# Folding batch 4's columns one step later: a limit table at the meeting of the transform stage and the expert slots

## Chip, cores and metric

One core of a Trainium2 chip runs the whole program. The metric is device time in microseconds (us), the median of several executions of the same kernel on the same inputs. An engine's queue is the list of its instructions in the order in which it takes them: PE (TensorE), DVE (VectorE), ACT (ScalarE), POOL (GpSimd) and SP (SyncE, which here only issues DMAs).

## What is computed

```python
def _attn_ref(x):                       # x: 8 batches of 2496 x 256
    X = np.fft.fft(x, axis=1)
    X = np.fft.fft(X, axis=2)
    return X.real.astype(np.float32)

def _moe_ref(x, w_gate, w_output_gate, w1, w2):   # x: the 19968 rows of the transform
    logits = x @ w_gate
    e_idx = np.argmax(logits, axis=1)             # one of 8 experts for each row
    ...
    for e in range(E):
        h = np.maximum(x[mask] @ w1[e], 0.0)
        ye = h @ w2[e]
        out[mask] = gate_w[mask, None] * eom[mask, e, None] * ye
```

The real part of a two-dimensional Fourier transform of each batch gives 2496 rows of 256. A gate picks one expert of eight for every row, and the expert is a two-layer network (256 to 1024 to 256).

## The kernel before

**The transform stage.** A batch's input comes as five column chunks, numbered m = 5 * batch + chunk (the code's `divmod(m, KC)`, KC = 5). Each chunk is a tile `xt` of 512 KB, loaded by SP (L310). `fold1` (L419) adds the two halves of a chunk in place. It runs on DVE for batches 0 to 3 and on POOL from batch 4 on; from batch 5 on it has two more POOL instructions (L424, L425). `fold2` then makes sums and differences on DVE: a difference `ft<-xt` (L437), a sum in place `xt<-xt` (L441), and for chunks 1, 3 and 4 two more (L450, L452). After L452 the tiles are free again and `load_x` puts the load of a later chunk into SP's queue. For batches from 4 on, `fold2` follows `fold1` two chunks later (FLAG = 2).

The steps of the transform are numbered n = 5 * batch + i. A step has `sstage` (L556 on PE, into PSUM tiles `psb_t`), then the call of `folds` that the change touches, then `sevac`, which reads the step's PSUM tile out: ACT writes `qb` (L580), DVE writes `eo` (L582) and `rt` (L587). Within some steps `dstage`/`devac` (L492, L504, L505) prepare the next batch. Rows of the finished transform go to a scratch array in HBM by scatters of POOL (L705).

**The slots.** The experts run in slots of up to 256 rows. A slot has four rounds: `mm1` (12 matmuls L1282 into a PSUM tile `hp`, then ACT `hh` L1286 and DVE `hl` L1287, the slot's subtraction) and, three rounds later, `mm2` (L1304 into `yp`). `hp` has two buffers, so the matmuls of a round wait for the `hl` of two rounds before. A slot's rows come by SP: a transposing load `xr` (L1214) and a small one `xf` (L1215). Its weights come as `raw0b`, `raw1b` (L1224) and are converted by ACT and DVE (L1258, L1259).

**How the two meet.** Steps n = 0 to 14 are written out ahead of the first slot (FSTART = 14). From step 15 on the steps are a background, cut into pieces that are drawn between the pieces of slots. In the background `fold2` is told to come behind the newest slot's subtraction (`behind("DVE")`), and it is interleaved with the gating of the previous batch. When step 14 is written the PSUM pools of the transform are closed, and the pools of the slots (`hp`, `yp`) take over the same PSUM. So the first `mm1` waits until step 14's `sevac` has read its PSUM tile.

SP and POOL take their instructions in the order in which the program writes them. The order on PE, DVE and ACT is set by the framework's scheduler, within what dependencies and a few pins allow; the folds ahead of the first slot are pinned in the program's order.

**The line that changes** is the call of `folds` at L1115. Its second argument is the last chunk to be folded in step n, the smallest of three limits. The third is a table, read by n - 10:

```python
min(KC * (b + 1) + AHEAD[i], KC + 3 * n + 2,
    KC * (BA + 1) + (1, 4, 5, 6, 9, 99)[min(n - 5 * BA, 5)])
```

With BA = 2 the table's base is 15, the first chunk of batch 3. Ahead of the first slot, a limit of 20 in step 12, 21 in step 13 and 24 in step 14 lets all five `fold1` of batch 4 (chunks 20 to 24) and the `fold2` of its first three chunks be issued there.

Of the kernel before, what the change touches and what calls it, by code (L numbers as in the profile page):

```python
# [19 lines left out]
KC = 5  # L20
# [21 lines left out]
BA = BAS[0]  # L42
# [26 lines left out]
AHEAD = (5, 6, 7, 8, 9)  # L69
# [164 lines left out]
def fft_moe_kernel(ctx: ExitStack, tc: tile.TileContext, xl, wg, w1, w2, tde, tdo, gt, ts0, tsm, tsr, tsq, cst, tid, out):  # L234
# [47 lines left out]
    if True:  # L282
# [18 lines left out]
        def load_x(n=NB * KC):  # L301

            while n and len(xq) < xcap[0]:
                q = pw if held[pw] < NX2 and len(xq) < 2 * KC else px
                if held[q] == (NX2 if q is pw else NX):
                    break
                held[q] += 1
                b, c = divmod(len(xq), KC)
                t = q.tile([128, 8, HN], F32, name="xt", tag="xt", bufs=NX2 if q is pw else NX)
                nc.sync.dma_start(t, xl[b, c])  # L310
                xts[b, c] = t
                xq.append(q)
                n -= 1
# [85 lines left out]
        def weave(*gs):  # L399
            gs = list(gs)  # L400
            while gs:
                for g in list(gs):
                    try:
                        next(g)
                    except StopIteration:
                        gs.remove(g)
# [4 lines left out]
        def fold1(b, c, eng):  # L411
            x = xts[b, c][:, :, 0:KW[c]]
            if b == 0:

                sq = pw.tile([128, 8, 128], mybir.dt.bfloat16, name="sq0", tag="sq0", bufs=1)
                nc.scalar.activation(sq[:, :, 0:KW[c]], x, AF.Square, scale=4.0, accum_out=en0[:, c:c + 1])
            v = x.rearrange("p (h a b) n -> p h a b n", h=2, a=2)
            x0, x1 = x[:, 0:4], x[:, 4:8]
            i = eng.tensor_tensor(x0, x0, x1, op=ALU.add)  # L419
            if b < LB:  # L420
                if eng is nc.vector:
                    pin(i)
                return
            eng.tensor_tensor(v[:, 1, 0], v[:, 0, 0], v[:, 0, 1], op=ALU.add)  # L424
            eng.tensor_tensor(v[:, 1, 1], v[:, 0, 0], v[:, 0, 1], op=ALU.subtract)  # L425
# [520 lines left out]
        def add_gen(g):  # L946
            gens.append([g, next(g)])
# [54 lines left out]
        def folds(n, last, fillers=None):  # L1002
            while fq[0] <= last:
                m = fq[0]
                fq[0] += 1
                dve = m // KC <= BA + 1
                if m < NB * KC:
                    fold1(*divmod(m, KC), nc.vector if dve else nc.gpsimd)
                while fq[1] < NB * KC and fq[1] <= m - (0 if fq[1] // KC <= BA + 1 else FLAG):
                    f = fold2(*divmod(fq[1], KC))  # L1010
                    fq[1] += 1
                    if n < 5 * BA or fillers is None:
                        weave(f)
                    else:
                        fillers.append(f)
# [31 lines left out]
        def scales(b):  # L1047
            smalls.clear()
            for fn in (energy, energy_sum, scale):
                fn(b)  # L1050

        def steps():
            pinned.append(1)
            folds(0, 2 * KC - 1)
            xcap[0] = NB * KC
            load_x()
            gatepass(0)
            add_gen(gating(0))
            for _ in sstage(0, 0):
                pass  # L1060
            weave(piece("C"), sevac(0, 0))
            scales(1)
            for m in range(2):
                for h in range(2):
                    load_w(0, m, h)
            weave(piece("A"))
            fa = foldall(BA)
            weave(piece("C"), dparts(1))
            weave(piece("C"))
            some(fa, 12)  # L1070
            for n in range(5 * BA):
                b, i = divmod(n, 5)
                if n:
                    for _ in sstage(b, i):
                        pass
                    for _ in sevac(b, i):
                        pass
                send(b, i)
                some(fa, 3 if n < 2 else 99)
                if n == 2:  # L1080
                    fq[:] = 2 * [KC * (BA + 1)]
                    gatepass(1)
                    add_gen(gating(1))
                ahead((0, 0, 8, 12, 99)[min(n, 4)])
                if n == 4:
                    for _ in table_a(0):
                        pass
                if n in (1, 2):
                    for h in range(2):
                        wenergy(0, n - 1, h)  # L1090
                if n == 4:
                    for m in range(2):
                        wscale(sched[0][1], m)
                if n > 7:
                    conv(0, 0, n - 8)
                yield ("step", n)
            for n in range(5 * BA, 5 * NB):
                b, i = divmod(n, 5)
                if i == 0 and b > BA:
                    add_gen(gating(b - 1))  # L1100
                smalls.clear()
                if n == 5 * BA:
                    hold.append(1)
                    scales(BA)
                    for c in range(KC):
                        dstage(BA, c)
                        devac(BA, c)
                ds_ = ((), (), (0, 1), (2, 3), (4,))[i] if b > BA else ((), (), (), (0, 1, 2), (3, 4))[i]
                for c in ds_ if b + 1 < NB else ():
                    dstage(b + 1, c)  # L1110
                    devac(b + 1, c)
                    yield "d"
                yield from sstage(b, i)
                fillers = [piece("C")] if i or b > BA else []
                folds(n, min(KC * (b + 1) + AHEAD[i], KC + 3 * n + 2, KC * (BA + 1) + (1, 4, 5, 6, 9, 99)[min(n - 5 * BA, 5)]), fillers)  # L1115
                weave(*fillers)
                yield "s"
                sv = sevac(b, i)
                next(sv)
                for _ in sv:  # L1120
                    pass
                if n == 5 * BA:
                    for h in range(2):
                        conv(0, 1, h)
                if i == 1 + (b == BA) and b + 1 < NB:
                    energy(b + 1)
                    energy_sum(b + 1)
                    scale(b + 1)
                weave(piece("A"))
                yield ("step", n)  # L1130
            add_gen(gating(NB - 1))
            while gens:
                for _ in piece("C"):
                    yield "g"
                yield "g"
                weave(piece("A"))
                yield "g"
# [400 lines left out]
```

## Time and profile before

| what | value |
|---|---|
| median of 3 runs | 1090.22 us (1090.05 to 1091.33) |
| the profiled execution | 1091.5 us |
| its span, first to last instruction | 1089.6 us |
| PE busy | 1035.8 us, 95% |
| DVE busy | 662.7 us, 61% |
| POOL busy | 419.8 us, 39% |
| mean granted TensorE clock | 0.983 |

Busy time is the time in which an engine works on an instruction. A row of a timeline has the start in us, the duration in us, the engine, the line and operation, the tiles written and read, the shapes, how many instructions it joins, and in brackets the idle time of the engine just before it with what ended that. Timelines join neighbours, so that a joined row's duration reaches from its first start to its last end. The granted clock is 1.00 at 2.4 GHz and 0.50 at 1.2 GHz.

### The profile page before, as it was taken

Reading aid. Unit: us, or ns where it says so; the run is one execution under the profiler, and the core shown is the slowest. Engines: PE = TensorE matmul, PEld = TensorE weight load, DVE = VectorE, ACT = ScalarE, POOL = GpSimd, SP = SyncE. Lnnn points to the kernel's source line nnn. Section 1 sums busy time; section 2 is a strip of 40 time slices with the busy share of each in tenths; the row PEclk is TensorE's granted clock in tenths of the full one; section 3 lists DMA queues with packets and bytes.
Section 4 is the critical chain, followed back from the end, with each engine's and each line's share of the span. In section 5 each row is a group of like instructions: output and inputs, shape, how many; then the busy total and the mean of one; then the engine's idle time right before and its main releaser. Section 6 shows DMA issues by size and latency. Waiting matters only on the chain. (4 is left out here: it accounts for less than half of the span.)

```text
span 1089.6 us, 27921 instructions
## 1 busy us (share of the span) xinstructions
PE 1035.8 (95%) x10226; PEld 931.1 (85%) x10226; DVE 662.7 (61%) x1356; ACT 599.8 (55%) x1099; POOL 419.8 (39%) x384
## 2 busy tenths in 40 slices
PE   5888499999999999999999999999999999999997
PEld 4686388889989999999998888888998989988996
DVE  6898576596787477466568545454446564545642
ACT  3486377676776456556553545544536554455552
POOL 0167325663773743535364752222121122112122
PEclk9899799999999999999999999999999999999999
DMA  9642645665575346556665895636647565474730
GB/s 359 208 169 88 215 127 155 170 184 145 166 196 146 109 126 165 136 141 169 153 162 117 223 198 155 156 80 198 148 111 195 157 173 136 121 204 126 187 79 24
DMA packets 152312, 171.02 MB, mean 157 GB/s; under 512 B 115309, under 2 KB 116207, under 8 KB 152164
## 3 DMA queue, kind: packets, MB, share of 16 engines
q1 hardware_dynamic: 136292, 126.48, 45.2%
q0 software_dynamic: 15728, 42.14, 11.6%
q8 instruction: 82, 1.34, 0.5%
q10 hardware_dynamic: 144, 0.52, 0.2%
q14 instruction: 66, 0.54, 0.2%
HBM read 149.51 MB, written 43.63 MB: 177 GB/s over the span
## 5 line engine op out<-in xcount | busy, mean ns | idle before, releaser
L1282 PE MATMUL hp<-xr,w0b 128*128 128x256 f16 (+2 forms) x4080 | 476.8, 266 | 20.5 <-DVE eo L582 14.7
L1304 PE MATMUL yp<-w1b,hh 128*128 128x256 f16 x2560 | 437.8, 273 | 0.0
L1282 PEld LDWEIGHTS <-w0b 128*128 128x128 f16 x4080 | 380.1, 98 | 61.8 <-DVE eo L582 14.9
L1313 POOL DMA_INDIRECT out_dram<-y,xf x160 | 186.3, 1165 | 537.0 <-ACT y L1312 491.9
L1304 PE MATMUL yp<-w1b,hl 128*128 128x256 f16 x1280 | 348.9, 273 | 0.0
L1287 DVE SCALAR_TENSOR_TENSOR hl<-hp,hh 128x512 f16<-128x512 f32 (+2 forms) x340 | 221.6, 654 | 197.9 <-ACT hh L1286 173.5
L1286 ACT ACTIVATE hh<-hp 128x512 f16<-128x512 f32 (+2 forms) x340 | 191.8, 567 | 246.1 <-PE hp L1282 244.0
L1304 PEld LDWEIGHTS <-hh 128*128 128x128 f16 x2560 | 248.2, 98 | 27.9 <-issue 0.2
L705 POOL DMA_INDIRECT scr<-rows,desti x160 | 173.6, 1085 | 101.2 <-DVE xt L441 49.1
L1304 PEld LDWEIGHTS <-hl 128*128 128x128 f16 x1280 | 125.3, 98 | 14.3
L1259 DVE SCALAR_TENSOR_TENSOR w0b<-raw0b,wsc,w0b 128x1024 f16<-128x1024 f32 x44 | 61.8, 1404 | 61.7 <-ACT w0b L1258 61.7
L1312 ACT ACTIVATE y<-yp,ysc 128x256 f32<-128x256 f32 (+1 forms) x160 | 67.5, 470 | 45.6 <-PE yp L1304 38.7
L1259 DVE SCALAR_TENSOR_TENSOR w1b<-raw1b,wsc,w1b 128x1024 f16<-128x1024 f32 x44 | 57.0, 1295 | 50.7 <-ACT w1b L1258 49.6
L1258 ACT ACTIVATE w0b<-raw0b,wsc 128x1024 f16<-128x1024 f32 x44 | 50.3, 1146 | 38.5 <-PE hp L1282 38.4
L492 PE MATMUL psb_t<-tdet,ft 128*125 128x290 f32 (+1 forms) x200 | 59.0, 448 | 13.1 <-DVE rt L575 5.3
L492 PEld LDWEIGHTS psb_t<-tdet,ft 128*125 128x125 f32 (+1 forms) x200 | 39.8, 208 | 27.1 <-issue 6.6
L1258 ACT ACTIVATE w1b<-raw1b,wsc 128x1024 f16<-128x1024 f32 x44 | 50.4, 1147 | 15.5 <-PE yp L1304 13.6
L1259 DVE SCALAR_TENSOR_TENSOR w1b<-raw1b,ssc,w1b 128x1024 f16<-128x1024 f32 x32 | 41.1, 1284 | 24.5 <-ACT w1b L1258 23.6
L1259 DVE SCALAR_TENSOR_TENSOR w0b<-raw0b,ssc,w0b 128x1024 f16<-128x1024 f32 x32 | 40.8, 1283 | 19.1 <-ACT w0b L1258 18.4
L505 DVE SCALAR_TENSOR_TENSOR alo<-psb_t,p_x,ahi 125x580 f16<-125x580 f32 (+1 forms) x40 | 32.4, 816 | 20.8 <-ACT ahi L504 20.7
L1258 ACT ACTIVATE w0b<-raw0b,ssc 128x1024 f16<-128x1024 f32 x32 | 36.4, 1145 | 11.3 <-DMA raw0b<-in_w_dram 10.3
L1258 ACT ACTIVATE w1b<-raw1b,ssc 128x1024 f16<-128x1024 f32 x32 | 36.7, 1145 | 9.8 <-DMA raw1b<-in_w_dram 9.0
(221 smaller groups left out, 984.3 us busy)
## 6 DMA issues: line engine op xcount, KB each, us to landing
raw0b<-in_w_dram SPq DMA_DIRECT2D x118, 512.0 KB
raw1b<-in_w_dram SPq DMA_DIRECT2D x118, 512.0 KB
xt<-in_xl_dram SPq DMA_DIRECT2D x40, 512.0 KB
scr<-rows,desti POOLq DMA_INDIRECT x160, 4.2
out_dram<-y,xf POOLq DMA_INDIRECT x160, 4.0
xr<-scr SPq DMA_TRANSPOSE x85
xf<-scr SPq DMA_DIRECT2D x75, 2.0 KB
tst<-in_ts_dram SPq DMA_DIRECT2D x2, 512.0 KB
```

The lines of the kernel that those rows point to most:

```text
L492: nc.tensor.matmul(o[:, 0:290], ft[:, k, par, W], tdab[:, k], start=(k == 0), stop=(k == 1))
L505: nc.vector.scalar_tensor_tensor(s["alo"][W, c], ps[W, :, 0:290], sc, s["ahi"][W, c], op0=ALU.mult, op1=ALU.subtract)
L705: free_order("scr", batch=b, inst=nc.gpsimd.indirect_dma_start(out=scr[:, :], out_offset=bass.IndirectOffsetOnAxis(ap=s["desti"][:, j:j + ...
L1258: nc.scalar.activation(w[:, 0], r, AF.Copy, scale=sc)
L1259: nc.vector.scalar_tensor_tensor(w[:, 1], r, sc, w[:, 0], op0=ALU.mult, op1=ALU.subtract)
L1282: nc.tensor.matmul(ps[:, k, T], w1v[:, hl, kc, (f % 4) * 128:(f % 4 + 1) * 128], a["x"][:, x, T], start=(m == 0), stop=(m == 5))
L1286: i = nc.scalar.activation(hh[:, G, T], ps[:, :, T], AF.Relu)
L1287: j = nc.vector.scalar_tensor_tensor(hl[:, G, T], ps[:, :, T], 0.0, hh[:, G, T], op0=ALU.max, op1=ALU.subtract)
L1304: nc.tensor.matmul(a["yp"][0:M, u], a[k, h][:, f, u * 128:u * 128 + M], w2v[:, hl, f], start=(g == 0 and f == 0 and m == 0), stop=(h == 1 ...
L1312: nc.scalar.activation(a["y"][0:M, u], a["yp"][0:M, u], AF.Copy, scale=ys[0:M, u:u + 1])
L1313: put = nc.gpsimd.indirect_dma_start(out=out[:, :], out_offset=bass.IndirectOffsetOnAxis(ap=a["f"].bitcast(I32)[0:M, u, 1:2], axis=0), in_ ...
```

## The change

The table gets one more entry and other values:

```diff
@@ -1112,7 +1112,7 @@
                 yield from sstage(b, i)
                 fillers = [piece("C")] if i or b > BA else []
-                folds(n, min(KC * (b + 1) + AHEAD[i], KC + 3 * n + 2, KC * (BA + 1) + (1, 4, 5, 6, 9, 99)[min(n - 5 * BA, 5)]), fillers)
+                folds(n, min(KC * (b + 1) + AHEAD[i], KC + 3 * n + 2, KC * (BA + 1) + (1, 4, 4, 4, 4, 9, 99)[min(n - 5 * BA, 6)]), fillers)
                 weave(*fillers)
                 yield "s"
```

Steps 12, 13 and 14 now fold nothing. Step 15, the first one in the background, gets all five `fold1` of batch 4 and the `fold2` of chunks 20 to 22; step 16 gets the `fold2` of chunks 23 and 24. Step 15 no longer folds chunk 25, which moves to step 16. No instruction is added or taken away.

On DVE, at the end of step 14 (ahead of the first slot) the order before is as follows, where `alo` is the last evacuation of batch 3's `dstage` and `eo` is step 14's read of PSUM:

```order
L505 SCALAR_TENSOR_TENSOR alo<-psb_t,p_x,ahi 128x580
L437 TENSOR_TENSOR ft<-xt 128x2x125 x3
L441 TENSOR_TENSOR xt<-xt 128x2x125 x3
L582 SCALAR_TENSOR_TENSOR eo<-psb_t,qb 128x290 x2
L450 TENSOR_TENSOR ft<-xt 128x2x125
L452 TENSOR_TENSOR ft<-xt 128x2x125
L587 TENSOR_TENSOR rt<-eo 128x2x129 x2
```

With the change, at the same place:

```order
L505 SCALAR_TENSOR_TENSOR alo<-psb_t,p_x,ahi 128x580
L582 SCALAR_TENSOR_TENSOR eo<-psb_t,qb 128x290 x2
L587 TENSOR_TENSOR rt<-eo 128x2x129 x2
L602 TENSOR_TENSOR lg<-qs 128x10x16
L604 TENSOR_TENSOR lg<-qs 128x10x16
```

The six instructions that stood between `alo` and `eo` are gone from there, and so are the two behind `eo`.

They are found again on DVE behind the fourth `hl`, in the first slot, with the change:

```order
L1287 SCALAR_TENSOR_TENSOR hl<-hp,hh 128x512
L437 TENSOR_TENSOR ft<-xt 128x2x125 x3
L651 TENSOR_TENSOR r_off<-psm_t,basem 128x8
L674 RECIPROCAL r_se<-r_se 128x20
L441 TENSOR_TENSOR xt<-xt 128x2x125 x3
L653 TENSOR_TENSOR basem<-psm_t,basem 128x8
L656 TENSOR_TENSOR r_t<-r_inc,r_off 128x160
L682 SCALAR_TENSOR_TENSOR car<-r_se,p_x,r_num 128x20
L450 TENSOR_TENSOR ft<-xt 128x2x125
L452 TENSOR_TENSOR ft<-xt 128x2x125
L1287 SCALAR_TENSOR_TENSOR hl<-hp,hh 128x512
```

Before, one L437, one L441, L450 and L452 (chunk 23) stood there, so two L437 and two L441 are new between these two `hl`.

On SP, behind the weight loads of the third slot, the order with the change is as follows (before, the first row had x7, the second row of `xt` loads x2 and the last x1):

```order
L310 DMA xt<-in_xl_dram 128x1024 x5
L1192 TENSOR_LOAD slots_a_69
L1192 ISA x2
L1214 ISA
L1214 DMA_TRANSPOSE xr<-scr 128x4x256
L1215 ISA
L1215 DMA xf<-scr 128x2x2
L310 DMA xt<-in_xl_dram 128x1024 x2
```

The loads of chunks 25 and 26 now stand behind the `xr` and `xf` of the third slot instead of ahead of them, and those of chunks 27 and 28 behind a weight load.

## Rows read from the trace of the kernel before

**Rows 1.** The page: busy time of each engine.

```profile
PE 1035.8 (95%) x10226; PEld 931.1 (85%) x10226; DVE 662.7 (61%) x1356; ACT 599.8 (55%) x1099; POOL 419.8 (39%) x384
```

**Rows 2.** Waits of PE, 110 to 140 us and 140 to 1090 us (total, times, longest).

```profile
PE hp L1282 <- DVE eo L582: 14.7, 1, 14.7
...
PE hp L1282 <- DVE hl L1287: 5.7, 5, 2.0
```

**Rows 3.** Timeline of DVE, 121 to 138 us.

```profile
121.42 0.82 DVE L505 SCALAR_TENSOR_TENSOR alo<-psb_t,p_x,ahi 128x580 f16<-128x580 f32 x1 [0.54 <-ACT ahi L504]
130.52 4.21 DVE L437 TENSOR_TENSOR ft<-xt 128x250 f32<-128x250 f32 x3 [8.28 <-POOL xt L419]
134.65 2.13 DVE L441 TENSOR_TENSOR xt<-xt 128x250 f32<-128x250 f32 x3
136.71 0.81 DVE L582 SCALAR_TENSOR_TENSOR eo<-psb_t,qb 128x290 f32<-128x290 f32 x2
```

**Rows 4.** Timeline of POOL, 122 to 150 us.

```profile
129.25 6.60 POOL L419 TENSOR_TENSOR xt<-xt 128x500 f32<-128x500 f32 x5 [15.87 <-issue]
142.56 1.25 POOL L419 TENSOR_TENSOR xt<-xt 128x500 f32<-128x500 f32 x1 [6.71 <-DMA xt<-in_xl_dram]
```

**Rows 5.** Timeline of SP, 60 to 170 us.

```profile
115.05 1.35 SPq L1214 DMA_TRANSPOSE xr<-scr  x1
...
122.14 17.80 SPq L310 DMA_DIRECT2D xt<-in_xl_dram  x7
140.71 1.27 SPq L1214 DMA_TRANSPOSE xr<-scr  x1
```

**Rows 6.** Timeline of ACT, 122 to 138 us.

```profile
122.94 0.41 ACT L580 ACTIVATE qb<-psb_t 128x290 f32<-128x290 f32 x1 [0.54 <-PE psb_t L556]
```

**Rows 7.** Timeline of PE: rounds of `mm1` in the first four slots.

```profile
137.58 2.74 PE L1282 MATMUL hp<-xr,w0b 128*128 128x256 f16 x12 [14.68 <-DVE eo L582]
...
154.92 1.47 PE L1282 MATMUL hp<-xr,w0b 128*128 128x256 f16 x12
...
167.81 0.49 PE L1282 MATMUL hp<-xr,w0b 128*128 128x256 f16 x3
...
178.97 1.47 PE L1282 MATMUL hp<-xr,w0b 128*128 128x256 f16 x12
```

**Rows 8.** Line 1282, 119 to 140 us: the weight loader's semaphore wait (ns min/median/max, first and last start).

```profile
L1282 PEldq EVENT_SEMAPHORE  x1: 51/51/51, 121.6 to 121.6; - x1
```

**Rows 9.** Windows: length, PE busy (instructions), granted clock, DMA share, GB/s.

```profile
122.50:123.00 0.50, 0.40 (x7) 1.00 0.86 344
127.50:128.00 0.50, 0.00 (x0) 0.64 1.02 418
133.00:133.50 0.50, 0.00 (x0) 0.50 0.44 172
141.00:141.50 0.50, 0.50 (x8) 0.71 0.76 295
239.50:241.50 2.00, 0.00 (x0) 1.00 0.26 104
241.50:242.50 1.00, 0.99 (x10) 1.00 0.64 123
```

**Rows 10.** Timeline of DVE: the fifth and the ninth `hl`.

```profile
152.00 0.69 DVE L1287 SCALAR_TENSOR_TENSOR hl<-hp,hh 128x512 f16<-128x512 f32 x1
...
166.35 0.68 DVE L1287 SCALAR_TENSOR_TENSOR hl<-hp,hh 128x512 f16<-128x512 f32 x1
```

**Rows 11.** DVE beside POOL: one difference, all of L437, all scans, one scan.

```profile
130.52 1.46 DVE L437 TENSOR_TENSOR ft<-xt 128x250 f32<-128x250 f32 x1 [8.28 <-POOL xt L419]
...
L437 DVE TENSOR_TENSOR ft<-xt x40: 403/415/1915, 9.2 to 420.9; 128x250 f32<-128x250 f32 x32, 128x256 f32<-128x256 f32 x8
...
L631 DVE TENSOR_TENSOR_SCAN r_inc<-cs,r_oh x8: 474/486/758, 42.5 to 567.9; 128x160 f32<-128x160 f32 x8
...
144.19 0.76 DVE L631 TENSOR_TENSOR_SCAN r_inc<-cs,r_oh 128x160 f32<-128x160 f32 x1
```

## The prediction

> **What bounds the kernel now.** I read the page's busy times first. PE works for 1035.8 of 1089.6 us and the next engine, DVE, for 662.7 [rows 1], so what can be won is idle time of PE, and each us of it taken away ahead of the slots moves everything behind it forward as long as PE stays busy there. Then the waits of PE. From 140 us to the end it waits in all some 6 us for `hl` [rows 2]; at the start of the first slot there is one wait of 14.7 us, for the `eo` of step 14. That is the largest one left, and it is where the change works.
>
> What holds that `eo` up is seen in DVE's timeline. `alo` ends at 122.24; then DVE is idle for 8.28 us, released by POOL's L419, does three L437 and three L441 until 136.78, and only then `eo` [rows 3]. Its own input `qb` was there from 122.94 + 0.41 = 123.35 [rows 6]. So `eo` is 13.36 us late for no reason of its own: it stands behind folds of batch 4. POOL starts those at 129.25 and works on the five until 135.85 [rows 4], since the chunks' loads are issued only from 122.14 on [rows 5], behind the first slots' rows and weights. From there the DMA share is near 1 until it falls to 0.44 in the half microsecond from 133.0 [rows 9]. The chain is load, POOL, DVE, PSUM read, first matmul.
>
> **The change, part by part.**
>
> *The stall goes.* With the six DVE instructions out of the way `eo` can start at 123.35. From its start to PE's first matmul it took 137.58 - 136.71 = 0.87 us [rows 3, 7], which gives 124.22 in place of 137.58: **13.4 us** won. PE ended its last matmul at 137.58 - 14.68 = 122.90, so 1.3 us of idle time stay.
>
> *What is late next.* The first matmul also needs its rows `xr`. The weight loader's own semaphore wait, which stands in front of it for that load, took 51 ns at 121.6 [rows 8], so the rows had landed by then, 2.6 us before they would be needed. The whole pile of transfers, the second slot's rows among it, has drained by about 133.5 [rows 9]. Six rounds took 154.92 - 137.58 = 17.3 us [rows 7], 2.9 us each, so the second slot's first round would start near 124.2 + 4 x 2.9 = 135.8. ACT's first look at the third slot's weights stands behind the third `hh`, an estimated 124.2 + 2 x 2.9 + 1.5 = 131.5. Those weights are the first in the pile, so I take no wait, and at most 2 us.
>
> *The clock.* During the idle time the granted clock fell from 1.00 to 0.50 (in 127.5 to 128.0), and it came back only in 141.0 to 141.5, to 0.71 on average over that half microsecond [rows 9]: 137.58 to 141.3 ran at 1.2 GHz, 3.7 us for work that takes half of that at 2.4 GHz. Does it still fall? The nearest row is an idle time of 2.03 us that ends at 241.5: the clock is 1.00 through it and after it [rows 9]. 1.3 us is shorter, so I take the **1.8 us** as won. The ends are 0 and 1.8.
>
> *What the slots have to bear.* The folds are still to be done. POOL's five L419 keep their hour: they wait for loads whose place in SP's queue has not changed. On DVE two more L437 and two more L441 stand between the fourth and the fifth `hl`. Alone an L437 takes 0.415 us (the median of forty [rows 11]), so about 4 x 0.41 = 1.65 us. The fifth `hl` ended at 152.69 and was needed by the seventh round's matmuls at 154.92 [rows 10, 7], so there are 2.2 us of slack, which covers this. But these L437 now also stand nearer to POOL. The fourth `hl` would come near 124.2 + 3 x 2.9 + 1.5 = 134.4, and the first three folds on POOL are done by 129.25 + 3 x 1.32 = 133.2; the last two run until 135.85. If DVE gets free of them only then, it needs about 4.9 us up to the end of the fifth `hl` (eight fold instructions at 0.41, `hl` 0.69, and five small ones estimated at 0.2), which is 140.8, against a seventh round due at 154.92 - 13.4 - 1.8 = 139.7: 1.1 us lost. In the next step the `fold2` of chunk 23 joins that of chunk 24 ahead of the ninth `hl`. It ended at 167.03 and its buffer was needed at 167.81 [rows 10, 7]: slack of 0.8 for 4 x 0.41 = 1.65 us more, so 0.85 us lost. The two don't add up in full, since a stall of PE gives DVE slack. Between 0 and 2.0 I take **1.0 us** lost.
>
> *SP and POOL.* The loads of chunks 25 and 26 go behind the third slot's `xr`. Before, SP stood at them until 139.94 and issued that `xr` at 140.71 [rows 5]; now it can issue it from about 124.6. The loads themselves wait for L452 of chunk 21, near 139 as before. Chunk 25's work on POOL started at 142.56 [rows 4]; it moves behind the first slot's two output scatters, and nothing needs it before the next batch's `fold2`. The loads of chunks 27 and 28 come behind the third slot's weight conversion, at the same time as before within a few us. I cost all of this at nothing. Its cover is that a batch's folds have about five steps until its `dstage`.
>
> *The sum.* 13.4 + 1.8 - 1.0 = 14.2 us. The profiled execution took 1091.5 us, so it would become 1077.3. The median of the runs shown is 1.3 us lower, and I forecast that: 1090.22 - 14.2 = **1076.0 us**. Behind the third slot the two kernels' instructions stand in the same order on all engines but for single neighbours, so what is won there should reach the end. The last matmuls and the tail behind them don't change.
>
> **The rivals.**
>
> *A. The folds contend with the slots.* One L437 beside POOL took 1.46 us and the three 4.21, where the median of all is 0.415 [rows 3, 11]: a DVE instruction that reads two SBUF tensors seems to wait for a POOL instruction's end. Until 135.85 POOL's folds now run beside the first slot. About six such DVE instructions (`r_oh`, scan, `r_zz`, two `rt`, `rows`) stand there; at 1.04 us more for each that is 6.2 us on DVE, less the slack of 2.2, so 4 us of PE. For it: the rows on L437. Against it: a scan that ran beside POOL's next chunk took 0.76 us against a median of 0.486 [rows 11], only 0.27 more, and six times that is within the slack. With 4 us lost the time is 1080.0. The Trainium skill's page "GPSIMD Engine Reference", section "Key points", states that GpSimd shares its SBUF interfaces with VectorE and contends with instructions that have two SBUF inputs. By that rule every one of the six pays, which is this rival in full; the L437 rows agree with it (1.46 against 0.415 us), the scan only in part.
>
> *B. Another release comes late.* If the first slot were held by something of the pile of transfers, it would start by 133.5 at the latest [rows 9]: 4.1 us won and nothing of the clock, 1086.1. Against it stands the 51 ns wait [rows 8].
>
> *C. The change doesn't do what it says.* If the PSUM tile that the first matmul takes over were held by something else on POOL's and DVE's chain, the wait would keep its length and the time would be 1090. The queues speak against it: nothing of the folds is left between `alo` and `eo`.
>
> *D. Slower: SP's queue.* The two `xt` loads that wait for L452 of chunk 21 now stand in front of the fourth slot's `xr` alone, with that L452 inside a slot. That slot's first matmul was at 178.97 [rows 7], so it is due near 163.8. The first slot's row load, issued at 115.05 [rows 5], had landed 6.6 us later [rows 8]. So from an L452 later than about 157 on, each us costs one us, and from 157 + 15.2 = 172 on the kernel is slower than before; at 175 it would be 1093. I expect 139. It takes a chain of waits of 33 us on DVE, which would need PE or a load to stand still too.
>
> **How the numbers follow.** The forecast, from 12.5 to 15.2 us won, has a chance of 0.66; A 0.18; B 0.08; C 0.04; D 0.04. The range begins at what no loss gives, 1090.22 - 15.2 = 1075.0, with 1 us for the scatter of runs (they lie 1.3 us apart), 1074. It ends at 1082, which takes in A with its bounds and some of the way to B; about 0.16 is left out. A measurement of this kernel can tell about 0.2%, 2.2 us, from no change. Faster by more than that are the forecast, A and B: 0.92. C is the same, 0.04; D is slower, 0.04.
>
> **What would show it.** In the new profile PE's wait for `eo` of 14.7 us is about 1.3 us long and the first `mm1` starts near 124; its twelve matmuls take 1.5 us instead of 2.74, at a clock of 1.00. DVE's `eo` follows `alo` with no idle time on POOL. In the first three slots there are at most small waits of PE for `hl`, and the rounds behind them come some 14 us earlier than before up to the end. The forecast is wrong if PE waits in the first slot for DVE for over 3 us (A), if the first matmul starts past 126 (B, C), or if it starts at 124 and the gain is gone by the fourth slot (D).

## The result, and the profile after

| what | before | after |
|---|---|---|
| median of 4 runs each, taken together | 1090.78 us (1090.05 to 1095.36) | 1080.81 us (1079.12 to 1081.76) |
| span of the profiled execution | 1089.6 us | 1079.0 us |
| mean granted TensorE clock | 0.983 | 0.991 |

The ratio of the times is 0.9906, with a 95% interval from 0.9887 to 0.9926. (Three of the four runs of before are those shown above; with the fourth their median is 0.6 us higher.) The changed kernel is 10.0 us faster; the forecast of 14.2 us was too large by 4.

The page, busy time of each engine after the change [rows 1 before]. The instructions are the same in number. PE is busy 2.2 us less, in part because its first matmuls are no longer slow (below); the rest of the gain is time that it no longer waits:

```profile
PE 1033.6 (96%) x10226; PEld 929.0 (86%) x10226; DVE 662.1 (61%) x1356; ACT 598.8 (55%) x1099; POOL 420.2 (39%) x384
```

The waits of PE after the change, 110 to 140 us and then 140 to 1090 us (total, times, longest), against [rows 2]:

```profile
PE hp L1282 <- DVE eo L582: 1.4, 1, 1.4
PE hp L1282 <- DVE hl L1287: 0.7, 1, 0.7
...
PE hp L1282 <- DVE hl L1287: 7.6, 6, 2.0
```

The 14.7 us are 1.4. But where there were 5.7 us of waits for `hl` in all, there are now 8.3. The timeline of PE shows which of them belong to the first four slots (the first round of `mm1`, the sixth, the eleventh, and a small product of the background), against [rows 7]:

```profile
123.53 1.48 PE L1282 MATMUL hp<-xr,w0b 128*128 128x256 f16 x12 [1.36 <-DVE eo L582]
...
136.31 1.47 PE L1282 MATMUL hp<-xr,w0b 128*128 128x256 f16 x12 [0.74 <-DVE hl L1287]
...
157.62 1.47 PE L1282 MATMUL hp<-xr,w0b 128*128 128x256 f16 x12 [1.99 <-DVE hl L1287]
...
161.12 0.38 PE L470 MATMUL psm_t<-es,cs 128*128 128x1 f32 x2 [1.05 <-DVE es L466]
```

The first round takes 1.48 us where it took 2.74. The granted clock says the same (windows after the change; the columns are length, busy time of PE, its weight loader, DVE, ACT and POOL, then the clock, the DMA share and GB/s), against [rows 9]:

```profile
122.50:123.50 1.00, 0.00 (x0) 0.00 (x0) 0.83 (x2) 0.11 (x1) 0.00 (x0) 1.00 1.01 414
123.50:130.00 6.50, 6.47 (x70) 5.99 (x71) 6.39 (x20) 4.33 (x9) 0.25 (x1) 1.00 1.02 407
130.00:138.00 8.00, 7.26 (x71) 6.45 (x69) 8.00 (x15) 5.31 (x12) 6.79 (x5) 1.00 0.77 165
```

Now DVE and POOL [rows 3, 4]. DVE's timeline after the change begins with `alo` and `eo`, with nothing of POOL between them; then, in the first slot, some instructions are much longer than elsewhere: the pair `rt`, `r_za`, `r_se` and the three L437.

```profile
120.68 0.82 DVE L505 SCALAR_TENSOR_TENSOR alo<-psb_t,p_x,ahi 128x580 f16<-128x580 f32 x1 [0.54 <-ACT ahi L504]
122.64 0.83 DVE L582 SCALAR_TENSOR_TENSOR eo<-psb_t,qb 128x290 f32<-128x290 f32 x2 [1.15 <-ACT qb L580]
...
130.07 2.60 DVE L587 TENSOR_TENSOR rt<-eo 128x258 f32<-128x258 f32 x2
132.59 0.68 DVE L1287 SCALAR_TENSOR_TENSOR hl<-hp,hh 128x512 f16<-128x512 f32 x1
133.20 0.62 DVE L646 SCALAR_TENSOR_TENSOR r_za<-r_z 128x20 f32<-128x20 f32 x1
133.74 0.69 DVE L590 TENSOR_TENSOR rows<-rt,rows 128x516 f16<-128x516 f32 x1
134.34 1.23 DVE L672 SCALAR_TENSOR_TENSOR r_se<-r_ez,r_se 128x20 f32<-128x20 f32 x1
...
136.18 1.54 DVE L437 TENSOR_TENSOR ft<-xt 128x250 f32<-128x250 f32 x3
```

The next lengthening is in step 16, between the eighth and the ninth `hl` (the same view, further on):

```profile
148.46 0.68 DVE L1287 SCALAR_TENSOR_TENSOR hl<-hp,hh 128x512 f16<-128x512 f32 x1
149.06 2.67 DVE L437 TENSOR_TENSOR ft<-xt 128x250 f32<-128x250 f32 x2
...
152.51 2.13 DVE L441 TENSOR_TENSOR xt<-xt 128x250 f32<-128x250 f32 x2
154.56 1.27 DVE L587 TENSOR_TENSOR rt<-eo 128x258 f32<-128x258 f32 x2
...
156.89 0.68 DVE L1287 SCALAR_TENSOR_TENSOR hl<-hp,hh 128x512 f16<-128x512 f32 x1
```

The timeline of POOL after the change has its folds at just these two places: batch 4's five from 129.75, and chunks 25 and 26 back to back from 149.34 (before, chunk 25 ran at 142.56 [rows 4], 19.5 us ahead of chunk 26):

```profile
129.75 7.04 POOL L419 TENSOR_TENSOR xt<-xt 128x500 f32<-128x500 f32 x5 [16.96 <-DVE r_zz L639]
149.34 1.26 POOL L419 TENSOR_TENSOR xt<-xt 128x500 f32<-128x500 f32 x1
...
152.27 1.24 POOL L419 TENSOR_TENSOR xt<-xt 128x500 f32<-128x500 f32 x1
```

**Where the time went.** The starts of the `hl` are a ruler, since every kernel here has the same ones in the same order. The lead of after over before is 15.8 us at the second `hl`, 12.7 at the eighth, 9.5 at the ninth, 11.0 at the seventeenth, and stays at 11.0 within 0.05 up to the 226th, at 820 us. In the spans it is 10.6. (820 us is the time in before.) So 15.8 us were won at the start, of which 0.7 are nothing of the change (the stage ahead ended that much sooner: `alo` at 120.68 and not 121.42). In the first four slots 4.8 were given back, where the forecast had 1.0.

### The profile page after: what moved, and what is told of

The parts are those of the page before. It is cut to its first block, busy times and chain, and to the rows that moved or that the text cites. A ratio compares the mean times of both kernels' runs of the same rounds, so it can differ in the third digit from the quotient of the medians.

```text
span 1079.0 us, 27924 instructions
## 1 busy us (share of the span) xinstructions
PE 1033.6 (96%) x10226; PEld 929.0 (86%) x10226; DVE 662.1 (61%) x1356; ACT 598.8 (55%) x1099; POOL 420.2 (39%) x384
## 3 DMA queue, kind: packets, MB, share of 16 engines
q8 instruction: 82, 1.34, 0.5%
## 5 line engine op out<-in xcount | busy, mean ns | idle before, releaser
L1259 DVE SCALAR_TENSOR_TENSOR w0b<-raw0b,wsc,w0b 128x1024 f16<-128x1024 f32 x44 | 61.7, 1403 | 58.1 <-ACT w0b L1258 58.1
L1259 DVE SCALAR_TENSOR_TENSOR w1b<-raw1b,wsc,w1b 128x1024 f16<-128x1024 f32 x44 | 56.9, 1294 | 50.6 <-ACT w1b L1258 49.5
L1259 DVE SCALAR_TENSOR_TENSOR w1b<-raw1b,ssc,w1b 128x1024 f16<-128x1024 f32 x32 | 41.0, 1283 | 24.7 <-ACT w1b L1258 23.0
L1259 DVE SCALAR_TENSOR_TENSOR w0b<-raw0b,ssc,w0b 128x1024 f16<-128x1024 f32 x32 | 40.8, 1282 | 20.0 <-ACT w0b L1258 19.3
```

The costliest lines, as they stand in the source:

```text
L1259: nc.vector.scalar_tensor_tensor(w[:, 1], r, sc, w[:, 0], op0=ALU.mult, op1=ALU.subtract)
```

## The experiments

Two theories of the 4.8 us. **Contention** (theory C in the expectations, not the rival C of the prediction): DVE's instructions are longer where POOL's folds run beside them, in the first slot and in step 16. **Own length** (theory Q): the folds put into the slots cost what their instructions take by themselves. Two more theories concern the gain: that the stall was the wait for POOL's first fold (S), and that the whole gain is a matter of how late POOL's folds are at the end of step 14 (R).

The ruler in all runs of which the start resembles the first measurement, in us between starts of `hl`, worked out from DVE's timelines:

| kernel | 2nd to 8th | 8th to 9th | 9th to 17th | 2nd to 17th |
|---|---|---|---|---|
| before | 17.5 | 5.2 | 31.1 | 53.9 |
| before, again (c_before) | 17.4 | 5.2 | 31.1 | 53.7 |
| after | 20.7 | 8.4 | 29.5 | 58.6 |
| after, again (c_after) | 20.7 | 8.4 | 29.5 | 58.7 |
| after, third time (f_after) | 20.9 | 8.4 | 29.5 | 58.9 |
| no POOL on 25, 26 | 20.9 | 4.6 | 29.9 | 55.4 |
| no POOL on 20 to 24 | 17.7 | 8.5 | 29.5 | 55.7 |
| 25, 26 a step later | 21.5 | 4.6 | 30.0 | 56.0 |
| five fold2 in step 15 | 27.2 | 1.3 | 30.4 | 58.9 |
| one fold2 ahead | 17.3 | 6.1 | 30.8 | 54.3 |

### What the slots pay for: POOL's folds left out or moved

**f_after**, the changed kernel as it is.

> The changed kernel as it is, as the reference of the three runs beside it. Expected as measured twice: about 1080 to 1084 us, first matmul of the slots some 14 us earlier than before; then 4.8 us lost in the first four slots: on DVE the pair rt (L587) of step 15 takes about 2.6 us, r_se (L672) about 1.2, the pair L437 of step 16 about 2.7 and the pair L441 about 2.1; PE waits 0.7 for the fourth hl, 2.0 for the ninth and 1.0 for es. From hl to hl: eighth to ninth about 8.4 us.

Measured: 1082.35 us (1079.63 to 1086.26, 6 runs), 0.990 of before (0.9872 to 0.9928; before took 1092.42 on this chip). The loss is there as expected, with one difference: in the first slot the pair `rt` took its normal 0.75 and the three L437 took 3.65 in its place. PE's wait came on `basem` (1.33), no longer on the fourth `hl`.

**f_no_pool_25_26** leaves out POOL's work on chunks 25 and 26:

```diff
-                if m < NB * KC:
+                if m < NB * KC and m not in (25, 26):
```

> POOL's work on chunks 25 and 26 (L419, L424, L425) is left out; the rest is the changed kernel. Theory C (POOL's folds beside DVE's cost the slots): the pairs L437 and L441 of step 16 take 0.74 us each and rt 0.77, the eighth hl to the ninth 4.6 us instead of 8.4, PE's waits of 2.0 (ninth hl) and 1.0 (es) are gone, and from the 17th hl on the kernel leads the changed one by about 2 to 3 us. Theory Q (the added DVE work by its own length, 4 x 0.41 us): all of these stay as in the changed kernel within 0.5 us. The first slot (rt 2.6, r_se 1.2, 0.7 us of wait) is unchanged under both.

Measured: step 16 in DVE's timeline,

```profile
151.61 0.68 DVE L1287 SCALAR_TENSOR_TENSOR hl<-hp,hh 128x512 f16<-128x512 f32 x1
152.21 0.74 DVE L437 TENSOR_TENSOR ft<-xt 128x250 f32<-128x250 f32 x2
...
153.73 0.74 DVE L441 TENSOR_TENSOR xt<-xt 128x250 f32<-128x250 f32 x2
154.39 0.76 DVE L587 TENSOR_TENSOR rt<-eo 128x258 f32<-128x258 f32 x2
...
156.20 0.68 DVE L1287 SCALAR_TENSOR_TENSOR hl<-hp,hh 128x512 f16<-128x512 f32 x1
```

The same instructions in the same order take 0.74 and 0.74 us instead of 2.67 and 2.13, the ninth `hl` follows the eighth after 4.59 us, and both waits of PE, 2.0 and 1.0, are gone. Against f_after, 3.5 us less pass from the second to the seventeenth `hl`, a little more than expected. In step 16 contention holds, and own length, which expects no change, falls. (The one run took 1076.84 us.)

**f_no_pool_20_24** leaves out POOL's work on chunks 20 to 24:

```diff
-                if m < NB * KC:
+                if m < NB * KC and m not in (20, 21, 22, 23, 24):
```

> POOL's work on chunks 20 to 24 (L419) is left out; the rest is the changed kernel. Theory C: in the first slot rt takes 0.77 us, r_se 0.17 and the three L437 0.42 each, PE's wait of 0.7 for the fourth hl is gone, and the second to the eighth hl take about 3 us less (19.5 to 20.5 in place of 23.4); step 16 (L437 2.7, L441 2.1) stays. Theory Q: the second to the eighth hl take within 0.5 us what they take in the changed kernel.

Measured, DVE's timeline in the first slot:

```profile
133.86 0.75 DVE L587 TENSOR_TENSOR rt<-eo 128x258 f32<-128x258 f32 x2
...
135.13 0.17 DVE L646 SCALAR_TENSOR_TENSOR r_za<-r_z 128x20 f32<-128x20 f32 x1
...
136.27 0.17 DVE L672 SCALAR_TENSOR_TENSOR r_se<-r_ez,r_se 128x20 f32<-128x20 f32 x1
...
137.05 1.06 DVE L437 TENSOR_TENSOR ft<-xt 128x250 f32<-128x250 f32 x3
138.30 1.00 DVE L441 TENSOR_TENSOR xt<-xt 128x250 f32<-128x250 f32 x3
```

Every one is back at its own length, and the stretch from the second to the eighth `hl` takes 17.7 us, 3.3 us less than in f_after, as expected (the figures given with it, 23.4 and 19.5 to 20.5, were 2.5 too high), and within 0.2 us of before. So the added L437 and L441, at their own length, cost the slots next to nothing: DVE's slack covers them. PE has no wait of over 0.2 us in the first slot. Step 16 stays as it was on DVE (PE's wait for the ninth `hl` is 0.5 us instead of 2.0). (One run, 1083.35 us; this execution reached its first `hl` 3.7 us later than f_after, so its time says nothing here.)

Together the two runs give back 3.5 + 3.2 = 6.7 us between the second and the seventeenth `hl`, where 5.0 had been lost (58.9 against 53.9). The kernel before paid for POOL in step 16 as well, for chunk 26 alone, and this went too: from the eighth to the seventeenth `hl` it takes 36.3 us, f_no_pool_25_26 34.5. The lines of before, the first from DVE's timeline and the second from POOL's:

```profile
161.71 1.91 DVE L437 TENSOR_TENSOR ft<-xt 128x256 f32<-128x256 f32 x1
162.07 1.26 POOL L419 TENSOR_TENSOR xt<-xt 128x500 f32<-128x500 f32 x1
```

**f_25_26_later** does all the work, but POOL's part on chunks 25 and 26 stands in step 17. Since `fold2` follows `fold1` two chunks later, a loop lets chunks 23 and 24 follow in step 16 all the same:

```diff
+            while n == 5 * BA + 6 and fq[1] < fq[0]:
+                fillers.append(fold2(*divmod(fq[1], KC)))
+                fq[1] += 1
...
-                folds(n, min(KC * (b + 1) + AHEAD[i], KC + 3 * n + 2, KC * (BA + 1) + (1, 4, 4, 4, 4, 9, 99)[min(n - 5 * BA, 6)]), fillers)
+                folds(n, min(KC * (b + 1) + AHEAD[i], KC + 3 * n + 2, KC * (BA + 1) + (1, 4, 4, 4, 4, 9, 9, 99)[min(n - 5 * BA, 7)]), fillers)
```

> All work is done; POOL's work on chunks 25 and 26 goes from step 16 to step 17, behind the fold2 of chunks 23 and 24. Theory C: step 16's pairs L437 and L441 take 0.74 us each, the ninth hl comes 3.5 to 4 us sooner, and the time is 2 to 3 us under the changed kernel beside it (about 1078), unless the same loss comes one step later, where POOL's work now stands beside step 17's few DVE instructions (then within 1 us of it). Theory Q: the same time as the changed kernel within 1 us.

Measured, DVE's timeline in step 16 and PE's one remaining wait for DVE in the slots up to 195 us (lines behind 1015 are three further down here):

```profile
150.37 0.74 DVE L437 TENSOR_TENSOR ft<-xt 128x250 f32<-128x250 f32 x2
```

```profile
138.11 1.47 PE L1285 MATMUL hp<-xr,w0b 128*128 128x256 f16 x12 [2.00 <-DVE hl L1290]
```

The loss of step 16 is gone and does not come back in step 17, where POOL now works without a break from 163.87 to 172.18. The first slot still pays, 21.5 us against 20.9 in f_after. From the second to the seventeenth `hl` it is 2.9 us less than in f_after, as expected. The time is 1080.84 us (1076.75 to 1085.18, 6 runs), ratio 0.9889 (0.986 to 0.9918): 1.5 us under f_after, and the intervals overlap. The trace has the gain up to 820 us; the medians do not settle it.

### Is the stall the wait for POOL?

**c_before** and **c_after** are the two kernels as they are, on one chip.

> The kernel before, unchanged, to have its trace beside the others on this chip. If the chip fetches PE's instructions as in the first measure, PE waits 14.7 us for eo ahead of the first slot and the time is near 1090. If it is one on which the transform stage is some 26 us longer, with PE idle on nothing but issue, as in the first four experiments, POOL has folded batch 4 before PE gets to the first slot: theory R (the gain is the lateness of POOL's folds against the end of step 14, no more) then expects the wait for eo to be below 4 us here.

> The changed kernel, unchanged. On a chip like that of the first measure: 1080.8, wait for eo 1.4 us, PE's waits in the first four slots 4 us. On a chip with the longer transform stage theory R expects the lead over the kernel before at the first hl to be what the wait for eo gives up there, below 4 us, and the ratio between 0.997 and 1.001; a theory in which the moved instructions are themselves worth the 11 us expects 0.99 there too.

Measured: 1092.34 us for the one run of c_before (1091.55 as the median of eleven beside it), and 1083.93 for c_after (1081.86 to 1088.36, 6 runs), ratio 0.9928 (0.99 to 0.9956). The two traces repeat the first ones: PE's wait for `eo` 14.7 and 1.4 us, in c_after the same waits of 0.8, 2.0 and 1.0 in the slots, and the same two stretches in the table. The start was the short one here, so theory R was not tested.

**e5_one_ahead** puts a part back ahead of step 14's `eo`: the `fold1` of chunks 20 to 22 and the `fold2` of chunk 20 alone, which is one L437 and one L441 where before had three each.

```diff
-... (1, 4, 4, 4, 4, 9, 99)[min(n - 5 * BA, 6)]
+... (1, 4, 4, 4, 7, 9, 99)[min(n - 5 * BA, 6)]
```

> The changed kernel with one of the three fold2 (chunk 20: one L437, one L441) put back ahead of step 14's eo. On a chip like that of the first measure, theory S (the stall is the wait for POOL's first fold, not the DVE work): eo waits for POOL's first L419, which ends near 130.5, then 1.5 us L437 and 0.8 to 1.5 us L441 beside POOL: first matmul at 132.5 to 134.5, so about two thirds of the 13.4 us come back with a third of the work. If the stall were the DVE work itself, a third of it would come back, first matmul near 128. On a chip with the longer transform stage: under 1 us later than in the changed kernel.

Measured, DVE's timeline and PE's:

```profile
130.61 1.47 DVE L437 TENSOR_TENSOR ft<-xt 128x250 f32<-128x250 f32 x1 [8.42 <-POOL xt L419]
132.11 1.34 DVE L441 TENSOR_TENSOR xt<-xt 128x250 f32<-128x250 f32 x1
```

```profile
134.24 2.74 PE L1282 MATMUL hp<-xr,w0b 128*128 128x256 f16 x12 [11.38 <-DVE eo L582]
```

With a third of the folds the wait is 11.4 us again, and the slow first round is back: 10.0 of the 13.3 us that the change had saved, in the range that theory S expected and not the third that the DVE work alone would give. DVE is idle for 8.42 us until POOL's first fold ends, as before [rows 3]; its two folds, 1.47 and 1.34 us beside POOL, make up the rest. So even one fold of batch 4 on DVE ahead of `eo` costs most of the stall.

The one run took 1094.89 us. It was 1.95 us ahead of c_before at the first `hl` and level with it at the 33rd. It lost 1.7 us of that between the 30th and the 32nd, where the granted clock was 0.50, from 240 to 243 us. PE had waited 2.02 us for an `hl`, until 238.50, and worked since. In c_before the same wait (2.04 us, until 240.16) left the clock at 1.00. First e5_one_ahead, then c_before (columns as in the windows above):

```profile
240.00:242.00 2.00, 2.00 (x11) 1.41 (x10) 1.97 (x5) 1.96 (x3) 0.00 (x0) 0.50 0.89 222
240.16:242.16 2.00, 2.00 (x20) 1.81 (x20) 1.57 (x6) 0.46 (x1) 0.00 (x0) 1.00 0.69 201
```

Of the ten traces in the table, eight keep 1.00 through and behind this wait; e5_one_ahead and f_no_pool_20_24 fall to 0.50 and lose 1.7 us each.

### All five fold2 in one step

**e4b_five_in_15** lets batch 4's `fold2` follow its `fold1` at once, so that all five stand in step 15 and none in step 16 beside chunks 25 and 26:

```diff
-                while fq[1] < NB * KC and fq[1] <= m - (0 if fq[1] // KC <= BA + 1 else FLAG):
+                while fq[1] < NB * KC and fq[1] <= m - (0 if fq[1] // KC <= BA + 2 else FLAG):
```

> All five fold2 of batch 4 in step 15, again, beside the changed kernel on the same chip. Theory C (contention in step 16): PE's waits between the 6th and the 12th hl are 2 to 3 us less than in the changed kernel, those in the first slot up to 1 us more, ratio to the changed kernel 0.998 to 0.9995. Theory Q: no difference.

Measured: 1082.28 us (1078.90 to 1085.97, 6 runs), ratio 0.9906 (0.9877 to 0.9934), not to be told from c_after. Contention had been expected to take 2 to 3 us off PE's waits between the 6th and the 12th `hl`; they are 2.8 us, where the changed kernel has 3.0. So that expectation was missed. DVE's timeline shows why: the five L437 stand beside POOL's last folds, and in step 16 `rt` and two weight conversions (L1259, 2.88 and 1.73 us where they take 1.28 elsewhere) now meet POOL's work on chunks 25 and 26:

```profile
136.84 4.32 DVE L437 TENSOR_TENSOR ft<-xt 128x250 f32<-128x250 f32 x5
...
149.36 2.88 DVE L1259 SCALAR_TENSOR_TENSOR w0b<-raw0b,wsc,w0b 128x1024 f16<-128x1024 f32 x1 [1.99 <-ACT w0b L1258]
...
153.61 2.23 DVE L587 TENSOR_TENSOR rt<-eo 128x258 f32<-128x258 f32 x2
```

From the second to the seventeenth `hl` it takes 58.9 us, as the changed kernel does. Here the eighth `hl` comes only at 157.49, behind these instructions, so that the ruler's first stretch holds both meetings with POOL (27.2 us) and the second next to nothing (1.3). Taking folds away from one meeting with POOL did not help, as long as others of DVE's instructions meet it.

### The same edits in a series where the whole start was longer

The first series ran at a time when the kernel before took 1138.86 us (1131.47 to 1143.5, 23 runs). The traces of its variants show the transform stage some 26 us longer, and PE's waits there (20 to 130 us, of e3_25_26_later) begin with "issue", time in which it waited for nothing that the profile shows. POOL's folds stand ahead of the first slot, whose first round was at 148.11 (POOL's timeline, the first three of five; the last ended at 145.86):

```profile
PE psb_t L556 <- issue: 14.8, 25, 1.2
```

```profile
138.10 3.78 POOL L419 TENSOR_TENSOR xt<-xt 128x500 f32<-128x500 f32 x3 [16.16 <-DVE rows L590]
```

**e1_no_pool_25_26**, **e2_no_pool_20_24** and **e3_25_26_later** have the edits of the three runs above (e1 and e2 leave out the same work, e3 does all of it); **e4_five_in_15** has that of e4b.

> The changed kernel with POOL's three fold1 instructions of chunks 25 and 26 left out (batch 5's first two columns stay unfolded); DVE's and PE's order stays that of the changed kernel. Theory C (contention: a DVE instruction that reads two SBUF tensors waits for POOL's instruction): in step 16 the two L437 take 0.8 us together instead of 2.67, the two L441 0.7 instead of 2.13, the two rt 0.8 instead of 1.27, the ninth hl comes 4 us sooner, PE's waits of 2.0 us (hl) and 1.05 us (es) go, and the lead over the kernel before at the 17th hl grows from 11.0 to some 14 us. Theory Q (queue length alone: the four more DVE instructions cost their own 0.41 us each, POOL has no part): durations and waits stay, the lead stays 11.0 us.

> The changed kernel with POOL's five fold1 instructions of batch 4 left out (batch 4's columns stay unfolded); DVE's and PE's order stays. Theory C: in the first slot the two rt take 0.8 us instead of 2.60 and r_se 0.2 instead of 1.23, the third to fifth hl come 2 to 3 us sooner, PE's wait of 0.74 us in the first slot goes, and the lead over the kernel before at the 6th hl is about 14.5 instead of 13.3 us; step 16 and its wait of 2 us stay as they are. Theory Q: durations stay, PE still waits 0.7 us, the lead at the 6th hl stays 13.3.

> The changed kernel with chunks 25 and 26 folded on POOL a step later (step 17), the fold2 of chunks 23 and 24 staying in step 16; all work is done. Theory C: step 16 runs without POOL beside it, as if the folds were left out: L437 pair 0.8 us, PE's wait for the ninth hl below 0.5 us, lead at the 17th hl 13 to 14 us unless step 17 pays for it, time 1077.5 to 1079 against 1080.8 of the changed kernel. Theory Q: the wait of 2 us stays, time 1080.8 within 0.5.

> The changed kernel with all five fold2 of batch 4 in step 15 (no lag of two chunks for batch 4), so that step 16 has only POOL's folds of chunks 25 and 26 and no fold2. Theory C: in the first slot four more DVE instructions of 0.35 us ahead of the fifth hl and four behind, PE waits there 1 to 2 us in all; in step 16 only eo and rt stand beside POOL, and the wait of 2 us for the ninth hl is below 0.5; lead at the 17th hl 12 to 13.5 us, time 1078 to 1080. Theory Q: the DVE work only changes its place, the sum of PE's waits in the first four slots stays 4 us within 0.5 and the time 1080.8 within 0.5.

Measured: step 16 gave the same answer as later. The pair L437 took 0.74 in e1 and e3 and 2.78 in e2, and the ninth `hl` followed the eighth after 4.59, 4.59 and 8.54 us. In the first slot leaving POOL's folds out could show nothing, since POOL was done before it: `rt` took 0.76 to 0.77 in e1, e2 and e3 alike, which is why the edits were run again. But e1 and e3 show the first slot with the added folds on DVE, all of batch 4's work done and POOL out of the way. In e3 DVE's three L437 take their own length:

```profile
157.86 1.07 DVE L437 TENSOR_TENSOR ft<-xt 128x250 f32<-128x250 f32 x3
```

The second to the eighth `hl` take 17.7 us in both, as in f_no_pool_20_24 and within 0.2 us of before. In e3, which meets POOL neither there nor in step 16 and does all the work, the second to the seventeenth take 53.7 us, as in before (53.9 and 53.7): nothing of the 4.8 is left, though in a series that was slower otherwise. Times: e1 1129.12 and e2 1141.33 us (one run each), e3 1137.88 (12 runs, ratio 0.9997, 0.9966 to 1.0027), e4 1139.07 (12 runs, ratio 1.0004, 0.9972 to 1.0035). In that series the two variants that do all the work gain nothing over before. That fits the reading that the gain is POOL's lateness at the end of step 14, which a longer stage ahead takes away; the changed kernel itself was not run in that series and no trace of before was taken there, so it stays a reading. What made that series longer stays open; that it was the fetching of PE's instructions, as the expectation of c_before supposes, no run shows.

## Why the prediction held, and where its sum was off

The range held (1074 to 1082, measured 1080.81), and so did the direction and the mechanism of the gain. The forecast proper, 12.5 to 15.2 us won, did not come: 10.0 were won, and the range held because it had been drawn to take in rival A. By its steps:

- **The stall goes: 13.4 us. Right.** PE's wait went from 14.68 [rows 7] to 1.36 us, 13.3 us, and the 1.3 us forecast as left are left. e5_one_ahead shows the chain: one fold in front of `eo` is enough to wait 8.4 us for POOL.
- **What is late next: nothing. Right.** No wait of PE for `xr` or weights is in the first slots. The weight loader's semaphore wait took 51 ns again, at 120.9 us [rows 8]. The `xt` loads that wait for L452 of chunk 21 were issued at 140.11, where 139 had been expected. The second slot's first round came at 133.44, not near 135.8: the 2.9 us a round were read from six rounds of which the first ran at 1.2 GHz.
- **The clock: 1.8 us. Right.** It is 1.00 in all windows from 122.5 to 138; 15.8 at the second `hl`, less 13.3 and the 0.7 of the earlier start, leaves 1.7 to 1.8. The row that spoke for it, an idle time of 2.03 us with the clock at 1.00, was less safe than it looked: two of ten traces fell to 0.50 behind that same wait (see e5_one_ahead). Behind the 1.36 us here none did.
- **What the slots have to bear: 1.0 us, between 0 and 2.0. Wrong in size: 4.8.** This is the step that failed, twice. The first time in the first slot: I priced the L437 and L441 behind the fourth `hl`, their wait for POOL included, and took the instructions ahead of them at their own length. Those paid most: in after, beyond their length elsewhere, `rt` 1.8, `r_za` 0.45, `r_se` 1.06 and the L437 0.5 us, together 3.8, of which the stretch up to the eighth `hl` shows 3.1 (20.7 against 17.5); in f_after the L437 paid 2.6 of 4.1. The second time in step 16: I priced the four fold instructions added there at 0.41 us each, as if POOL were idle. It worked on two chunks, and the stretch grew by 3.2 us (8.4 against 5.2; 4.6 without POOL). 1.6 us came back up to the seventeenth `hl` (29.5 against 31.1), and 3.1 + 3.2 - 1.6 is the 4.8 but for rounding. This term explains the whole miss: 14.2 - 3.8 is 10.4, and the lead of 11.0 less the 0.7 of the earlier start is 10.3. The added folds' own length, the part that I had worked out with care, costs next to nothing: without POOL beside it the first stretch takes what it took before, within 0.2 us.
- **SP and POOL at nothing. Right for SP, wrong for POOL.** I asked who needs chunk 25 (nobody, for five steps) and not what it stands beside. The change moved it from 142.56, where it met little, to 149.34, next to chunk 26 and beside step 16's folds. (The runs left out or moved both chunks together, so the share of chunk 25 alone is not shown.) A row that prices this was in the argument: the longest L437 before, 1915 ns in [rows 11], is step 16's L437 beside chunk 26, shown above at 161.71. I read the median of that row and not its maximum.
- **Rival A** gave 1080.0 us and the time came out there, by its mechanism, though at other places: `r_oh`, the scan and `r_zz` were over before POOL began, and step 16 was not in it. By the sign set for it, a wait of PE for DVE of over 3 us in the first slot, it did not come: that wait was 0.7 us, and much of the loss lay in step 16. The evidence I set against A, one scan at 0.76 us, was a poor witness: at 144.19 it met the rest of a short POOL instruction, L424, which ended at 144.60, and not folds of 1.25 us back to back.
- **Rivals B, C and D.** The first matmul came at 123.53 and not past 126 (B, C); the lead did not shrink at the fourth slot but grew from 9.5 to 11.0 us there (D).
- **What reaches the end.** 11.0 us as far as 820 us, 10.6 in the spans. The forecast was of a median 1.3 us under the profiled execution; the median of after is just 0.1 us from its profiled execution's 1080.72.

## What to carry to other kernels

When work of one engine is moved, ask of it not only who needs it and who it delays in its queue, but which instructions of other engines run beside it at its new hour; here that was where the loss came from, and step 16's share of it stood beside POOL work whose move had been costed at nothing. Where an engine's instruction has a maximum far over its median, look the maximum up: it names the neighbour. And before pricing a moved instruction by its own length, see whether the slack there covers that length; in the first slot here it did, and only the contention counted.

## What the runs showed of the hardware

**A DVE instruction with two inputs in SBUF and a POOL `tensor_tensor` take turns.** The timelines of the changed kernel in narrow windows, so that the joined rows come apart: POOL's folds, and then DVE's two `rt` (with `hl`, `r_za`, L590 and `r_se` above).

```profile
129.75 1.25 POOL L419 TENSOR_TENSOR xt<-xt 128x500 f32<-128x500 f32 x1 [16.96 <-DVE r_zz L639]
130.96 1.43 POOL L419 TENSOR_TENSOR xt<-xt 128x500 f32<-128x500 f32 x1
132.35 1.43 POOL L419 TENSOR_TENSOR xt<-xt 128x500 f32<-128x500 f32 x1
133.74 1.80 POOL L419 TENSOR_TENSOR xt<-xt 128x500 f32<-128x500 f32 x1
```

```profile
130.07 1.21 DVE L587 TENSOR_TENSOR rt<-eo 128x258 f32<-128x258 f32 x1
131.20 1.47 DVE L587 TENSOR_TENSOR rt<-eo 128x258 f32<-128x258 f32 x1
```

The first `rt` ends at 131.28, 0.3 us behind POOL's first fold (131.00); the second at 132.67, 0.3 behind the second (132.39); `r_za` at 133.82, just behind the third (133.78). Then L590, which began with POOL's fourth, took its normal 0.69, and POOL's fourth took 1.80 instead of 1.25; `r_se`, twenty elements, waited until 135.57 for POOL's end at 135.54. So an instruction that has to wait waits for the other engine's current one to end, however short it is itself: 0.17 us became 1.23. The Trainium skill, page "SBUF — State Buffer", section "SBUF: two separate sides", says that VectorE and GpSimd share a port pair as an exclusive lock, which a VectorE instruction with two SBUF inputs wants against a GpSimd one that reads SBUF, and that whoever starts first keeps it for the whole instruction while the other blocks. The blocking in these rows agrees with it. `hl`, which reads one of its inputs from PSUM, took 0.68 us beside POOL and without it.

Who gets the turn can't be read from the recorded starts. In step 16 the first L437 starts 0.28 us ahead of POOL's L419 (149.34, above) and still ends 0.29 behind it, at 150.88:

```profile
149.06 1.82 DVE L437 TENSOR_TENSOR ft<-xt 128x250 f32<-128x250 f32 x1
```

The L437 of before did the same with chunk 26 (161.71 against 162.07), and the L1259 of e4b_five_in_15 began at 149.36, 0.54 ahead of POOL's L419 at 149.90, and paid 1.6 us. By recorded starts these three don't fit "whoever starts first" in that sentence of the Trainium skill; why stays open.

**Which instruction pays changes from run to run, the sum less so.** What the long ones of the first slot took beyond their own length was 3.8 us in after and in c_after (`rt`, `r_za`, `r_se`, L437), 4.1 in f_after (`r_za` 0.45, `r_se` 1.05, the L437 3.65 - 1.06 = 2.6) and 4.6 in f_25_26_later (`rt`, `r_za`, `r_se` and `r_num`, L677).

**The last rounds scatter.** Up to the 226th `hl`, at 820 us, the traces of the changed kernel keep the same distances within 0.3 us. Behind that, the traces of the two kernels as they are drift apart by up to 3 us, and those of all runs by more. The one wait of PE that differs much there, for the queue of DVE at the weight conversion L1257, was 0.4 us in after, 2.8 in c_after, 2.4 in f_after and 3.5 in c_before, and there was none in before. In c_before and e5_one_ahead the clock also fell to 0.50 there, from 983 us on for some 3 us. So 3 us seen in a trace can be lost in medians of six runs.
